# Random-feature attention and a normalised two-layer MLP on one core: tokens centred in place of weights, fp32 weight loads, shared PSUM banks, half-array products and a backward-pass order

## The chip, the cores and the metric

The kernel runs on one core of one Trainium2 chip. The metric is device microseconds (us) from launch to end. Five engines work from lists in fixed order: TensorE (PE; its weight loads are shown as PEld), VectorE (DVE), ScalarE (ACT), GpSimd (POOL) and SyncE (SP, which here only issues DMAs). The lists are made when the program is built. Nothing is reordered at run time: an instruction that waits holds up all that stands behind it on its engine.

## The reference, cut to what matters

```python
def phi(x):                                            # x: (8, 8, 576, 64)
    proj = np.einsum('bhsd,df->bhsf', x, w_phi)        # w_phi: (64, 128)
    proj = proj - np.max(np.abs(proj), axis=-1, keepdims=True)
    return np.concatenate([np.exp(proj), np.exp(-proj)], axis=-1)
q_p, k_p = (phi(q), phi(k))
kv = np.einsum('bhsf,bhsd->bhfd', k_p, v); z = np.sum(k_p, axis=2)
num = np.einsum('bhsf,bhfd->bhsd', q_p, kv)
den = np.einsum('bhsf,bhf->bhs', q_p, z)[..., None] + 1e-06
x = num / den                                          # heads side by side: (8, 576, 512)
xn = (x - mean(x)) / np.sqrt(var(x) + 1e-06) * g_ln
out = x + np.maximum(xn @ w_ch1, 0.0) @ w_ch2          # 512 -> 2048 -> 512
```

## The kernel before, in words

**Attention** goes in 32 units; a unit is two (batch, head) slices. Its 1152 rows are eight tiles of 128 plus a ninth, "mixed", tile that holds the two 64-row tails. For one unit PE transposes k and q into `qkT_ps` (L397, and the mixed tile in L405), multiplies by w_phi into `pm` (L476: four products of 256 columns for k, four for q; the weight is block-diagonal, so that one product serves two slices) and into `px` for the mixed tile (L433, L434). It multiplies q once more with the features on the partitions into `pt` (L543). DVE takes the largest absolute value over the features (L483, L437), ACT the exponentials (L492 for k, L549 for q, L447 and L451 for the mixed tile). POOL scales v by the maxima's exponentials into `vv` (L504 to L513). PE sums `kv` (L571, L576) and `num` (L605, L611). DVE combines the two halves of `num` and inverts the denominator (L618, L624, L628), and POOL writes the quotient into `x` (L634).

**MLP.** Eight units make a pair: two batches with all heads, so 1152 rows of x. A pair goes through the MLP in three blocks of 384 rows: PE transposes x (`xT_ps`, L705), multiplies by `w1` (`hT_ps`, L776, 16 groups of four products per block), ACT or DVE apply the relu (L786, L784; every third group is DVE's by a fixed rule), PE multiplies by `w2` (`ch_ps`, L807), DVE scales by 1/std and adds x (L814), SP stores.

**Mean.** The mean of the layer norm is taken out of the weights: for each quarter n of w1, PE makes the mean over the rows (`mean_ps`, L346), ACT copies it (L353), DVE scales by g and subtracts (L356, L363) and POOL subtracts for two of four row blocks (L368). The transposed x can then be used uncentred.

**Loads.** q, k, v come by SP's queue in fp32. The bf16 transposes read the upper halves of the fp32 words. w1 and w2 come in quarters by POOL's queue, which turns fp32 to bf16 on the way (L310, L320). Each quarter's issue stands on POOL behind the `vv` work of one unit (`behind`).

**PSUM** has eight banks: `ps_A` two buffers of two banks (pm and pt; after pair 0 also qkT_ps and px), `ps_N` one bank (kv, num), `ps_B` three banks (hT_ps, ch_ps, xT_ps, mean_ps; in pair 0 also qkT_ps and px).

**Order.** The program first lists all operations with an engine, an estimated duration, a hand-made rank (a planned start time `V`) and what they read and write. `Order.run` then plays the list through: each engine takes the ready operation of lowest rank. What comes out is the order in which instructions are emitted.

Of the kernel before, what the change touches and what calls it, by code (L numbers as in the profile page):

```python
# [22 lines left out]

class Op:
    __slots__ = (
        "engine", "us", "emit", "rank", "lag", "deps", "users", "acquire", "release",
        "ready", "left", "number",
# [3 lines left out]
class Order:  # L31

# [9 lines left out]
    def add(self, engine, us, rank, emit, r=(), w=(), acquire=None, release=None, lag=0.12):  # L42
        op = Op()
        op.engine, op.us, op.emit, op.rank, op.lag = engine, us, emit, rank, lag
        op.acquire, op.release = acquire, release
        op.number, op.users, op.ready = len(self.ops), [], 0.0
# [11 lines left out]
        return op  # L58

    def run(self):  # L60
        waiting, free, room, events, done = {}, {}, self.room, [], []

        def offer(op):
            heapq.heappush(events, (op.ready, 1, op.number, op))

        for op in self.ops:
            waiting.setdefault(op.engine, [])
            free.setdefault(op.engine, 0.0)
            if not op.left:
                offer(op)  # L70
        now = 0.0
        while events:
            now = events[0][0]
            while events and events[0][0] <= now + 1e-9:
                _, kind, _, op = heapq.heappop(events)
                if kind == 1:
                    heapq.heappush(waiting[op.engine], (op.rank, op.number, op))
                elif kind == 0:
                    if op.release:
                        room[op.release[0]] += op.release[1]  # L80
            for engine, queue in waiting.items():
                if free[engine] > now + 1e-9 or not queue:
                    continue
                passed = []
                while queue:
                    item = heapq.heappop(queue)
                    op = item[2]
                    if op.acquire is None or room[op.acquire[0]] >= op.acquire[1]:
                        break
                    passed.append(item)  # L90
# [3 lines left out]
                if op is None:  # L94
                    continue
                if op.acquire:
                    room[op.acquire[0]] -= op.acquire[1]
                end = now + op.us
                free[engine] = end
                done.append(op)  # L100
                heapq.heappush(events, (end, 2, op.number, op))
                heapq.heappush(events, (end + op.lag, 0, op.number, op))
                for o in op.users:
                    o.ready = max(o.ready, end + (0.03 if o.engine == engine else op.lag))
# [4 lines left out]
        for op in done:  # L109
            if op.emit:  # L110
                op.emit()
# [4 lines left out]
def kernel(  # L116
# [11 lines left out]

# [21 lines left out]
    ST = NT * P  # L150
# [7 lines left out]
    NR = ST // RN  # L158
    NM = RN // P
    NW = 4  # L160
    WC = DH // NW

# [3 lines left out]
    xpool = ctx.enter_context(tc.tile_pool(name="xpool", bufs=NPAIR))  # L166
    moe_sb = ctx.enter_context(tc.tile_pool(name="moe_sb", bufs=2))
    out_pool = ctx.enter_context(tc.tile_pool(name="out_sb", bufs=4))

    ps_A = ctx.enter_context(tc.tile_pool(name="ps_A", bufs=2, space=bass.MemoryType.PSUM))  # L170
    ps_N = ctx.enter_context(tc.tile_pool(name="ps_N", bufs=1, space=bass.MemoryType.PSUM))
    ps_B = ctx.enter_context(tc.tile_pool(name="ps_B", bufs=3, space=bass.MemoryType.PSUM))


    wphi_f = consts.tile([P, F], FP32, name="wphi_f")
    nc.sync.dma_start(out=wphi_f[0:D, :], in_=w_phi)
    nc.sync.dma_start(out=wphi_f[D : 2 * D, :], in_=w_phi)
    gln_sb = consts.tile([P, KC], FP32, name="gln")

    ident = consts.tile([P, P], BF16, name="ident")  # L180
    make_identity(nc, ident)
    nc.scalar.preload_act_table_set("natural_log_exp_and_others")

    wb = {}
    for nm, s0, s1 in (("wbk", 1.0, 1.0), ("wbx", 2.0, 1.0), ("wbq", 2.0, 2.0)):
        wb[nm] = t_ = consts.tile([P, 2, F], BF16, name=nm)
        nc.vector.memset(t_, 0.0)  # L190
        nc.vector.tensor_scalar_mul(out=t_[0:D, 0, :], in0=wphi_f[0:D, :], scalar1=s0)
        nc.vector.tensor_scalar_mul(
            out=t_[D : 2 * D, 1, :], in0=wphi_f[D : 2 * D, :], scalar1=s1
        )
    wbq, wbk, wbx = wb["wbq"], wb["wbk"], wb["wbx"]

    eps_sb = consts.tile([P, 1], FP32, name="eps")
    nc.vector.memset(eps_sb, 1e-6)
    ones = consts.tile([P, P], BF16, name="ones")
    nc.vector.memset(ones, 1.0)  # L200

    qk_bufs, v_bufs = [], []
    for i in range(NBUF):
        qk_bufs.append((
            consts.tile([P, 2, HG, MX * D], FP32, name=f"qk{i}"),
            consts.tile([P, HG, 2, D], FP32, name=f"qx{i}"),
        ))

        vx = consts.tile([P, HG, 2, D1], FP32, name=f"vx{i}")
        nc.gpsimd.memset(vx, 0.0)  # L210
        nc.gpsimd.memset(vx[0:64, :, 0, D:D1], 1.0)
        nc.gpsimd.memset(vx[64:128, :, 1, D:D1], 1.0)
        v_bufs.append((consts.tile([P, HG, MX * D], FP32, name=f"v{i}"), vx))
# [3 lines left out]
    ea_bufs = []  # L217
    for i in range(2):
        eb = consts.tile([P, 2, (MX + 2) * P], BF16, name=f"ea{i}")
        nc.gpsimd.memset(eb[:, :, MX * P :], 0.0)  # L220
        ea_bufs.append(eb)

    w1_sb = consts.tile([P, KC, DH], BF16, name="w1")
    w2_sb = consts.tile([P, JC, DM], BF16, name="w2")

    g_mean = consts.tile([P, KC, P], BF16, name="g_mean")

    sched = Order({"A": 2, "N": 1, "B": 3})
    add = sched.add

    def mm(n, cols):
        return n * (cols / 2.4 + 4.0) / 1000.0


    GBPS = 215.0

    behind = []

    def dma(queue, rank, nbytes, emit, r=(), w=(), us=0.6, lag=2.2):
        r = (*r, *behind)  # L240
        key = ("dma", len(sched.ops))
        add(queue, us, rank, emit, r=r, w=(key, *w))
        add("DMA", nbytes / GBPS / 1000.0, rank, None, r=(key, *r), w=w, lag=lag)

    def load_group(g, rank, units, queues):

        (qk, qx), (vb, vx) = qk_bufs[g % NBUF], v_bufs[g % NBUF]
        pair, hg = divmod(g, NGRP)
        u0, nu = units[0], len(units)
        us = slice(u0, u0 + nu)  # L250

        def rows(t, half, tail):
            if pair == 0:
                b, h0, step = hg // 2, 4 * (hg % 2) + 2 * u0 + half, 2
            else:
                b, h0, step = 2 * pair + half, hg * HG + u0, 1
            run, np_, s0 = (D, 64, 4 * P) if tail else (4 * D, P, 0)
            return bass.AP(
                tensor=t.tensor, offset=t.offset + ((b * H + h0) * S + s0) * D,
                ap=[[run, np_], [step * S * D, nu], [1, run]],  # L260
            )

        def rows_of_pair(t):
            b, h0 = hg // 2, 4 * (hg % 2) + 2 * u0
            return bass.AP(
# [693 lines left out]
```

## Time and profile before

| | |
|---|---|
| median of 2 runs (433.11 and 434.84) | 433.98 us |
| span of the profiled execution, first to last instruction | 431.2 us |
| busy PE, DVE, ACT, POOL in it | 385.5, 302.7, 234.1, 170.8 us |
| mean granted TensorE clock | 0.956 |
| last `ch_ps` product ends | 426.7 us |

The profile has no time of its own for the profiled execution outside its span; the median stands 2.8 us above it, which is taken as what lies around the span. Products of PE overlap in the pipeline: the duration of one runs from its entry to its last result, so what a row of products costs in a full stream is read from the distance between the starts of neighbouring rows.

### The profile page before, as it was taken

To read this page: it belongs to the slowest core of one execution; us is meant where nothing else is said; L and a number is where in the kernel's file an instruction comes from. 1 tells how busy PE (TensorE), PEld (TensorE's weight loads), DVE (VectorE), ACT (ScalarE), POOL (GpSimd) and SP (SyncE) were. 2 spreads that over 40 slices of the span, in tenths; PEclk is the share of its full clock that TensorE was granted. 3 is DMA by queue.
4 is the path that set the end of the run, shared out by engine and by line. 5 is a ranking of instruction groups with operands and counts; after the bars stand their busy time and mean duration, and the time that the engine had idled before them with its cause. 6 is when DMAs were issued, how large, how long until landed. Compare 5 with 4: busy or idle time off the path is not lost.

```text
span 431.2 us, 9039 instructions
## 1 busy us (share of the span) xinstructions
PE 385.5 (89%) x3340; PEld 242.6 (56%) x3392; DVE 302.7 (70%) x727; ACT 234.1 (54%) x513; POOL 170.8 (40%) x345
## 2 busy tenths in 40 slices
PE   3755657899999999799999999999999999999995
PEld 2532533565666666566666666666666655555542
DVE  4787788678878787797687887888778869322222
ACT  1863452777576664666566665577567741522210
POOL 2758674577044354640344444434444520000000
PEclk9985677999999999699999999999999999999999
DMA  5999493375332424511244243510100011101012
GB/s 143 220 271 244 134 228 114 49 120 149 128 110 81 136 87 154 142 53 52 85 123 143 81 135 106 160 55 2 42 34 2 26 49 51 27 24 49 26 49 73
DMA packets 50732, 42.67 MB, mean 99 GB/s; under 512 B 17280, under 2 KB 46080, under 8 KB 50688
## 3 DMA queue, kind: packets, MB, share of 16 engines
q1 hardware_dynamic: 45072, 37.30, 28.2%
q0 software_dynamic: 4224, 4.19, 6.1%
q10 hardware_dynamic: 1392, 0.59, 0.6%
q8 instruction: 26, 0.43, 0.4%
q14 instruction: 18, 0.15, 0.1%
HBM read 36.77 MB, written 9.44 MB: 107 GB/s over the span
## 4 chain that ended last, share of the span: by engine, by line
PE 81%; DVE 6%; ACT 6%; issue 2%; DMA 2%; POOL 2%; SPq 1%; ACTq 0%; DVEq 0%; POOLq 0%
PE hT_ps L776 29%; PE ch_ps L807 27%; PE pm L476 6%; PE kv L576 4%; PE num L605 3%; PE qkT_ps L397 3%; ACT ea_129 L549 3%; PE pt L543 2%; PE xT_ps L705 2%; DVE w_133 L356 2%; PE mean_ps L346 1%; PE kv L571 1%; DVE m L483 1%; ACT EB L492 1%; PE num L611 1%
## 5 line engine op out<-in xcount | busy, mean ns | idle before, releaser
L776 PE MATMUL hT_ps<-xT,w_133 128*128 128x384 bf16 x768 | 148.9, 328 | 4.6 <-DVE hT L784 1.9
L807 PE MATMUL ch_ps<-w_134,hT 128*128 128x512 bf16 x539 | 142.7, 379 | 1.8
L786 ACT ACTIVATE hT<-hT_ps 128x384 bf16<-128x384 f32 x132 | 65.1, 493 | 85.4 <-PE hT_ps L776 85.0
L634 POOL TENSOR_TENSOR x<-numc,rden 128x192 bf16<-128x192 f32 (+3 forms) x112 | 51.3, 461 | 135.6 <-DVE rden L628 125.3
L776 PEld LDWEIGHTS <-w_133 128*128 128x128 bf16 x768 | 73.0, 98 | 55.2 <-issue 6.5
L483 DVE TENSOR_REDUCE m<-pm 128x8 f32<-128x1024 f32 x64 | 77.9, 1218 | 15.3 <-PE pm L476 14.6
L807 PEld LDWEIGHTS <-hT 128*128 128x128 bf16 x576 | 51.9, 98 | 41.7
L784 DVE TENSOR_SCALAR hT<-hT_ps 128x384 bf16<-128x384 f32 x60 | 33.3, 555 | 41.3 <-PE hT_ps L776 41.0
L492 ACT ACTIVATE EB<-pm 128x1024 bf16<-128x1024 f32 x64 | 62.2, 1025 | 0.0
L618 DVE TENSOR_TENSOR numc<-num,em 128x195 f32<-128x195 f32 x96 | 33.9, 353 | 18.9 <-PE num L605 10.3
L814 DVE SCALAR_TENSOR_TENSOR o<-ch_ps,rstd,x 128x512 f32<-128x512 f32 x36 | 26.8, 746 | 19.2 <-PE ch_ps L807 19.2
L549 ACT ACTIVATE ea_129<-pt 128x1024 bf16<-128x1024 f32 x32 | 32.0, 1022 | 11.4 <-PE pt L543 6.0
L549 ACT ACTIVATE ea_131<-pt 128x1024 bf16<-128x1024 f32 x32 | 32.2, 1033 | 7.4 <-PE pt L543 4.9
L624 DVE TENSOR_TENSOR numc<-numc,num 128x195 f32<-128x195 f32 x96 | 33.9, 353 | 1.9
L476 PEld LDWEIGHTS <-qkT 128*128 128x128 bf16 x256 | 24.4, 103 | 14.1 <-issue 5.9
L447 ACT ACTIVATE EB<-px 128x128 bf16<-128x128 f32 x64 | 17.8, 278 | 24.1 <-DVE m L437 22.0
L415 DVE COPY qkT<-qkT_ps 128x1024 bf16<-128x1024 bf16 x32 | 21.8, 681 | 9.6 <-PE qkT_ps L397 9.3
L576 PE MATMUL kv<-vv,EB 128*128 128x65 bf16 x512 | 28.3, 201 | 0.0
L576 PEld LDWEIGHTS <-EB 128*128 128x128 bf16 x512 | 24.1, 103 | 3.7 <-issue 0.5
L728 DVE BATCH_NORM_STATS2 st<-x 128x6 f32<-128x512 bf16 x36 | 24.4, 678 | 0.0
L476 PE MATMUL pm<-wbk,qkT 128*128 128x256 bf16 x128 | 21.3, 294 | 2.8 <-DVE qkT L415 1.1
L476 PE MATMUL pm<-wbq,qkT 128*128 128x256 bf16 x128 | 20.6, 286 | 2.9 <-ACT ea_129 L549 2.2
(95 smaller groups left out, 509.1 us busy)
## 6 DMA issues: line engine op xcount, KB each, us to landing
out_dram<-o SPq DMA_DIRECT2D x32, 256.0 KB, 2.3
qk_108<-in_k_dram SPq DMA_DIRECT2D x10, 256.0 KB, 3.2
v_114<-in_v_dram SPq DMA_DIRECT2D x10, 256.0 KB, 3.3
w_133<-in_moe_w_ch_dram POOLq DMA_DIRECT2D x4, 512.0 KB, 8.0
qk_115<-in_k_dram SPq DMA_DIRECT2D x8, 256.0 KB, 3.4
qk_115<-in_q_dram SPq DMA_DIRECT2D x8, 256.0 KB, 3.2
qk_122<-in_k_dram SPq DMA_DIRECT2D x8, 256.0 KB, 2.9
v_121<-in_v_dram SPq DMA_DIRECT2D x8, 256.0 KB, 2.9
```

Of the source, the lines that this page charges most:

```text
L476: nc.tensor.matmul(ps[:, 2 * c : 2 * c + 2, :], u["qkT"][:, (i * 4 + c) * P : (i * 4 + c + 1) * P], wbk if i else wbq, start=True, stop=True,)
L483: nc.vector.reduce_max(out=u["m"][:, i, 0:MX], in_=u["pm", i], axis=AX.X, apply_absolute_value=True)
L492: nc.scalar.activation(u["EB"][:, t, 0:MX, :], u["pm", 1], AF.Exp, scale=(1.0, -1.0)[t])
L549: nc.scalar.activation(u["EA"][:, t, 0:1024], u["pt"], AF.Exp, scale=(1.0, -1.0)[t])
L576: nc.tensor.matmul(ps[:, t, c // 4, :], EB[:, t, c, :], vv[:, t, c, :], start=False, stop=(t == 0 and c == MX - 1), skip_group_check=True,)
L618: nc.vector.tensor_tensor(out=st["numc"], in0=st["ps"][:, 1], in1=bcast(u["em", 0][:, c0 : c0 + 3], 2, D1), op=ALU.mult,)
L624: nc.vector.tensor_add(out=st["numc"], in0=st["numc"], in1=st["ps"][:, 0])
L634: nc.gpsimd.tensor_tensor(out=dst, in0=st["numc"][ps_, i : i + n, 0:D], in1=bcast(st["rden"][ps_, i : i + n], 2, D), op=ALU.mult,)
L776: nc.tensor.matmul(st["ps"], w1_sb[:, kc, jj * P : (jj + 1) * P], pr["xT"][r][:, kc, :], start=(kc == 0), stop=(kc == KC - 1),)
L784: nc.vector.tensor_relu(h_sb, st["ps"])
L786: nc.scalar.activation(h_sb, st["ps"], AF.Relu)
L807: nc.tensor.matmul(ch[t], hT[r, jj][:, rt * P : (rt + 1) * P], w2_sb[:, jj, :], start=(jj == 0), stop=(jj == JC - 1),)
```

## The change

**Tokens centred.** `mean_ps`, its copy and the centring of w1 go. DVE instead subtracts the mean from each 128-row tile of x (`xc`, L841; 36 of them) once `bn_stats` has given it, and PE transposes xc. The transposes now stand behind the statistics.

**Weights.** The eight quarters come as fp32 by SP's queue into the buffers of x that pairs 2 and 3 use later (`stage`, two of them), and ACT or POOL cast 32 pieces of 128x512 to bf16; those of w1 are multiplied by g on the way. A quarter's load waits for the casts of the quarter two before it.

**Loads of tails.** The 64-row tails of q, k, v come for four or eight units at once, before for one or two. The first DMA is k's main rows, before it was w_phi and tails.

**Mixed tiles** are done once for two units of k, and for two units of q, with products of their own (L400 to L459). In pair 0, where a unit is two heads of one batch, the tails of both batches are joined in one mixed tile in the second half of the pair. The small copies `x<-xs` by DMA go.

**Half-array products.** `pm` is now made by products with 64 rows: each tile of 128 rows is multiplied by the 64x128 w_phi once on the upper and once on the lower half of the array (L543), into different banks. A unit has 16 products of 128 columns, before 8 of 256.

**PSUM.** `ps_A` stays with two buffers of two banks for pm and pt. The other four are one pool of single banks, for all else. `pm` for k and q are one operation after pair 0.

**Engines by choice.** The copies of qkT_ps and xT_ps and all relus may go to ACT or DVE, whichever the planner has free first.

**Ranks.** `Order.due` plays the list backward from the end, by due times; the rank of an operation is its due time less an allowance (8 us for attention, 4 us for transposes and statistics, 0 for the MLP). Durations and delays between engines in the planner are new.

```diff
+        for op in self.ops:
+            op.rank = rank[op.number] - op.early
...
+            nc.vector.tensor_scalar(
+                out=pr["xc", r][:, t % NM, :], in0=x[:, t, :],
+                scalar1=pr["mv"][:, t, 0:1], scalar2=None, op0=ALU.subtract,
+            )
...
+            for i in sides:
+                u["pm", i] = ps = ps_A.tile([P, 2, MX // 2, F], FP32, tag="A", name="pm")
+                for c in range(4):
+                    for e in range(2):
+                        rows = slice(e * D, (e + 1) * D)
+                        nc.tensor.matmul(
+                            ps[:, e, c, :],
+                            u["qkT"][rows, (i * 4 + c) * P : (i * 4 + c + 1) * P],
+                            (wbk if i else wbq)[rows, e, :], start=True, stop=True,
+                        )
...
+                if e == "ACT":
+                    nc.scalar.activation(dst, src, AF.Copy, scale=g)
+                else:
+                    ENG[e].tensor_scalar_mul(out=dst, in0=src, scalar1=g)
...
+    ps_B = ctx.enter_context(tc.tile_pool(name="ps_B", bufs=4, space=bass.MemoryType.PSUM))
...
+    load_w1(0, "SP", 1.6)
+    load_w1(1, "SP", 2.6)
```

Three places in the lists, before and now. On PE, before, between the two halves of the `kv` of unit 2, counted from 0 (x is the attention's result, w_133 is w1, qk_122 the third group of q and k loads, that of units 4 and 5):

```order
L705 MATMUL xT_ps<-ident,x 128x128
L346 LDWEIGHTS g_mean
L346 MATMUL mean_ps<-w_133,g_mean 128x512 [waits DMASW0_49]
...
L571 LDWEIGHTS EB
L571 MATMUL kv<-vv,EB 128x130 [waits Pool_49]
...
L405 LDWEIGHTS qx_123 [waits DMAHW3_49,DMAHW7_49,DMAHW2_49,DMAHW0_49]
L405 MATMUL qxT_ps<-ident,qx_123 128x128
L397 LDWEIGHTS qk_122 [waits DMAHW1_49]
```

and now, where the third group is called qk_84:

```order
L694 MATMUL num<-KV,ea_95 128x65
L513 LDWEIGHTS qk_84 [waits DVE_49,DMAHW5_49]
L513 MATMUL qkT_ps<-ident,qk_84 128x128 [waits PE_49]
...
L658 LDWEIGHTS EBx
L658 MATMUL kv<-vv,EBx 128x130 [waits Pool_49]
...
L513 LDWEIGHTS qk_84 [waits DMAHW6_49]
```

The transposes of unit 4 stood behind two groups of mean products, the `num` of unit 2 and the first half of the `kv` of unit 3; now they stand behind the `num` of unit 1, around the second half of the `kv` of unit 2, and no product waits for w1 there. The first `hT_ps` product stood at row 686 of 6786, when the `pm` of six units were issued; it now stands at row 1054 of 7266, when those of eight units are issued and unit 8 is transposed.

The loads. Before on POOL, a quarter of w1 behind each unit's `vv`:

```order
L513 TENSOR_TENSOR vv<-vx_110,en 128x130
L310 DMA w_133<-in_moe_w_ch_dram 128x4x512
L504 TENSOR_TENSOR vv<-v_114,em 128x8x64
L509 CAST vv<-em 128x8
L513 TENSOR_TENSOR vv<-vx_110,em 128x130
```

and now on SP (x_102 and x_103 are the two staging buffers, qk_83 and v_86 the loads of group 1, those numbered 84 and 87 of group 2, qk_82 of group 3):

```order
L275 DMA qk_83<-in_q_dram 128x2x256
L275 DMA x_102<-in_moe_w_ch_dram 128x4x512
L275 DMA v_86<-in_v_dram 128x2x256
L275 DMA x_103<-in_moe_w_ch_dram 128x4x512
L275 DMA qk_84<-in_k_dram 128x4x256
L275 DMA qk_84<-in_q_dram 128x4x256
L275 DMA kx_90<-in_k_dram 64x4x64 x2
L275 DMA v_87<-in_v_dram 128x4x256
L275 DMA vx_92<-in_v_dram 64x4x64 x2
L275 DMA qx_88<-in_q_dram 64x8x64 x2
L275 DMA qk_82<-in_k_dram 128x4x256
```

The weights are in one queue with q, k and v, and the first half of w1 stands ahead of the loads of units 4 to 7. The casts stand on POOL and ACT between the work of the units:

```order
L614 TENSOR_TENSOR vv<-vx_92,en 128x130
L359 TENSOR_SCALAR w_98<-x_102,gln 128x512 x2
L605 TENSOR_TENSOR vv<-v_86,emk 128x8x64
L610 CAST vv<-emk 128x8
L614 TENSOR_TENSOR vv<-vx_92,emk 128x130
```

A cast that waits for its load holds up the `vv` behind it.

More of the change, by code (lines that the diff above doesn't have):

```diff
@@ L198 @@
[L198 to L213, printed above, removed]
@@ L228 @@
-    sched = Order({"A": 2, "N": 1, "B": 3})
-    add = sched.add
-    def mm(n, cols):
[L232 to L240, printed above, removed]
-        key = ("dma", len(sched.ops))
[L242 to L248, printed above, removed]
+    x_bufs = [consts.tile([P, NT, DM], BF16, name=f"x{i}") for i in range(NPAIR)]
@@ new lines, in tails @@
+        data = []
+        for what in parts:
+            for s in range(n0, n0 + 2) if what == "k" else qheads:
+                data += tail_keys(pair, s, what)
+        key = (g, slot)
+        pool, tag, res = bank(g)
+        wide = ns * 2 * F + (2 * P if qheads else 0)
+        add("PE", mm(ns, 128), V, transposes, r=data, w=[("xT2_ps", key), ("xT2", slot % 2)],
+            acquire=("B", 1))
+        add_any(
+            {"DVE": 0.13 + ns * 0.07, "ACT": 0.1 + ns * 0.11}, V, copy,
+            r=[("xT2_ps", key)], w=[("xT2", slot % 2)], release=[("B", 1)],
+        )
@@ L647, in a_num @@
[L647 to L655 removed]
+                out=dst, in0=st["numc"][:, i : i + cnt, 0:D],
+                in1=bcast(st["rden"][:, i : i + cnt], 2, D), op=ALU.mult,
+            )
+        key, s = ("num", num), num % 3
+        n_mm = sum(2 if c.__defaults__[0] else 1 for c in chunks) * 2
@@ L912 @@
[L912 to L925 removed]
+            w_ = units[n - 1]
```

1093 lines of the change are left out of this document (650 added, 443 removed).

## The prediction

> **What bounds the kernel now.** I read the page's busy times and slices first, then the windows by stage, then the timeline of each stage, and last the chain.
>
> ```profile
> span 431.2 us, 9039 instructions
> PE 385.5 (89%) x3340; PEld 242.6 (56%) x3392; DVE 302.7 (70%) x727; ACT 234.1 (54%) x513; POOL 170.8 (40%) x345
> PE   3755657899999999799999999999999999999995
> PEclk9985677999999999699999999999999999999999
> ```
>
> PE is the busiest engine. The digits show two kernels in one: up to the eighth slice, some 80 us, PE is half idle and for part of it at a reduced clock; from there it is full, except near slice 17. The windows, cut at those stages, say the same (the columns are busy us and count of PE, PEld, DVE, ACT, POOL, then clock, DMA share, GB/s):
>
> ```profile
> 0.00:28.80 28.80, 15.29 (x151) 11.10 (x154) 19.91 (x52) 16.16 (x34) 15.78 (x43) 1.00 0.83 207
> 28.80:47.70 18.90, 10.57 (x82) 6.29 (x82) 13.15 (x28) 6.21 (x12) 14.10 (x24) 0.51 0.82 212
> 47.70:80.00 32.30, 21.54 (x187) 14.31 (x190) 25.70 (x56) 16.79 (x39) 19.73 (x35) 0.81 0.68 160
> 200.00:366.00 166.00, 164.38 (x1527) 104.94 (x1552) 130.98 (x324) 101.08 (x224) 66.61 (x132) 1.00 0.22 71
> ```
>
> From 200 to 366 us PE is busy 99% of the time at full clock. To see whether busy is also full, I read the distance of the starts there:
>
> ```profile
> 324.72 0.61 PE L397 MATMUL qkT_ps<-ident,qk_108 128*128 128x128 bf16 x8
> 325.17 0.81 PE L776 MATMUL hT_ps<-xT,w_133 128*128 128x384 bf16 x4
> 325.82 0.22 PE L571 MATMUL kv<-vv,EB 128*128 128x130 bf16 x1
> 325.88 0.42 PE L576 MATMUL kv<-vv,EB 128*128 128x65 bf16 x8
> 326.13 0.81 PE L807 MATMUL ch_ps<-w_134,hT 128*128 128x512 bf16 x3
> 326.78 0.22 PE L571 MATMUL kv<-vv,EB 128*128 128x130 bf16 x1
> 326.84 0.42 PE L576 MATMUL kv<-vv,EB 128*128 128x65 bf16 x8
> 327.09 0.60 PE L476 MATMUL pm<-wbq,qkT 128*128 128x256 bf16 x4
> 327.53 0.59 PE L543 MATMUL pt<-qkT,wbk 128*128 128x512 bf16 x2
> 327.96 0.33 PE L705 MATMUL xT_ps<-ident,x 128*128 128x128 bf16 x3
> ```
>
> One product follows the next in a distance that goes with its columns: 0.056 us for 128 (325.17 less 324.72, by 8), 0.1625 for 384, 0.217 for 512, 0.11 for 256, 0.031 for 65, 0.06 for 130. So from 80 us on only fewer products, or fewer columns, make the kernel shorter. The start is another matter:
>
> ```profile
> 10.00 2.36 DVE L483 TENSOR_REDUCE m<-pm 128x8 f32<-128x1024 f32 x2
> 25.60 1.23 DVE L483 TENSOR_REDUCE m<-pm 128x8 f32<-128x1024 f32 x1
> 33.40 1.39 DVE L363 TENSOR_SCALAR w_133<-w_133,gln 128x512 bf16<-128x512 bf16 x2
> 41.37 3.14 DVE L356 SCALAR_TENSOR_TENSOR w_133<-w_133,gln,mean 128x512 bf16<-128x512 bf16 x2
> 48.95 1.23 DVE L483 TENSOR_REDUCE m<-pm 128x8 f32<-128x1024 f32 x1 [0.67 <-PE pm L476]
> 65.35 1.44 PE L776 MATMUL hT_ps<-xT,w_133 128*128 128x384 bf16 x4 [1.25 <-DVE xT L711]
> 79.51 1.46 PE L776 MATMUL hT_ps<-xT,w_133 128*128 128x384 bf16 x8 [0.48 <-DVE hT L784]
> ```
>
> The first maxima of units 0 and 3 start at 10.0 and 25.6 us: 5.2 us a unit, with DVE as the pace. The next unit's come at 48.95, after a hole of 23 us in which DVE centres w1 and PE's list is at the mean products, with unit 4's transposes behind them. MLP products start at 65.35 and run without holes from 79.5.
>
> **The change part by part.** I sum the new span in four pieces: up to the first hT product, the products after it, the idle time among these, the end.
>
> *The start.* The mean products, their copies and the centring go, and with them the hole. What remains is the attention's pace. The first load is now k's, so I let the first maximum come 2.5 us earlier, at 7.5. Eight units have their pm before the first hT: 8 x 5.2 = 41.6. Added to DVE in this stretch are three tiles' statistics and centrings and three copies of xT_ps. Their rows, and those that I need below:
>
> ```profile
> L728 DVE BATCH_NORM_STATS2 st<-x 128x6 f32<-128x512 bf16 x36 | 24.4, 678 | 0.0
> L729 DVE BATCH_NORM_AGGREGATE mv<-st 128x2 f32<-128x6 f32 x36 | 6.5, 182 | 1.2
> L363 DVE TENSOR_SCALAR w_133<-w_133,gln x8: 341/447/1252, 33.4 to 71.6; 128x512 bf16<-128x512 bf16 x8
> L786 ACT ACTIVATE hT<-hT_ps 128x384 bf16<-128x384 f32 x132 | 65.1, 493 | 85.4 <-PE hT_ps L776 85.0
> L711 DVE COPY xT<-xT_ps 128x384 bf16<-128x384 bf16 x48 | 16.5, 347 | 6.3 <-PE xT_ps L705 6.2
> L434 PE MATMUL px<-qkT,wbk 128*128 128x128 bf16 x32 | 7.5, 233 | 0.0
> DMA packets 20847, 15.14 MB, mean 189 GB/s; under 512 B 7402, under 2 KB 20840, under 8 KB 20840
> 426.68 0.75 DVE L814 SCALAR_TENSOR_TENSOR o<-ch_ps,rstd,x 128x512 f32<-128x512 f32 x1 [2.48 <-PE ch_ps L807]
> ```
>
> That is 3 x (0.678 + 0.182 + 0.447) + 3 x 0.347 = 5.0 (a centring is the form of L363, whose median I take; its bounds are 0.34 and 1.25, or 1 us less and 2.4 more). By the engines the first hT comes at 7.5 + 41.6 + 5.0 = 54 us. Half of the qkT copies may go to ACT; the casts (six on ACT, ten on POOL in this stretch, no row shows them in this form) fall on engines that were busy 16 of the first 29 us, so I let them cost nothing here; without this cover, six on ACT would be 3 us at the 0.493 of L786, which is the nearest in size.
>
> But the loads now share one queue, in a fixed order: up to the last quarter of w1, whose cast stands on ACT and POOL inside unit 7, SP and ACT issue 14.0 MB (7.1 of q, k and v of pair 0, 4.2 of w1, the rest for units 8 to 11). At the 189 GB/s of the first 80 us (row above) that lands at 74 us, at the 290 of the best ten us before (row under rival b) at 48; behind the cast stand some 6 us of ACT's work before the first hT. So the loads say 54 to 80, the engines 54. I take **62**: nearer the engines, because the rate before included stretches in which the queue waited.
>
> *The products after it.* Behind the first hT the list holds 768 hT (124.8 us at 0.1625), 576 ch (125.0 at 0.217), 896 of 65 columns (27.8), 48 of 130 (2.9), 48 pt (10.4 at 0.217), 363 transposes and px of 128 (20.3), 23 px of 256 (2.5) and 384 pm of 128 (21.5). Sum 335. Only the last group is of a new kind. Before, these 24 units had 192 products of 256 (21.1 us): if the halves ran one after another, nothing would be gained. If two run side by side, a pair costs at least one 0.056, and at most two weight loads with their products as they pass at 65 columns, 2 x 0.031 = 0.062. I take 0.062: 192 x 0.062 = 11.9, or **9.6 less** (bounds 10.8 less and none). The change from whole to half array and back, twice for each of 24 blocks, may cost nothing, or as much as a product stays in the array beyond its distance: 0.233 (L434) less 0.056 = 0.177. I take the middle, 0.1: **4.8** (0 to 8.5).
>
> The Trainium skill (TensorE: Matmul & The Clock Gate, Part 3 on packing small matmuls) has products on different row groups run together, 4 ns apart; its page TensorEngine Tiling (Key Properties) has every change of tiling mode drain the array. No run so far shows either. By both together the two terms would be 10.8 less and 8.5 more, which makes 412 instead of the sum below.
>
> *Idle among them.* Before, from the 25th hT product at 79.51 to the end of the last ch at 426.7 is 347.2 us, for products that add up to 335.0 by the same distances: 12 us idle. Most of it lay between pairs 1 and 2, where x is not yet complete:
>
> ```profile
> 160.00:200.00 40.00, 35.96 (x337) 23.99 (x341) 33.91 (x85) 25.31 (x56) 17.15 (x34) 0.91 0.37 109
> ```
>
> The change puts statistics and centring into that chain, and against it spreads the MLP products by due times: by the distances above, the lists now hold 10 us of MLP products between the first pm of units 15 and 16 and 11 between those of 16 and 17; before they held 2 and none. I take **10** (4 to 18). PE stays the bound there: DVE was busy 131 of 166 us from 200 on (fourth row of the windows); 36 centrings at 0.447 add 16 us to its whole list, and about half of the qkT copies leave it.
>
> *The end* is unchanged: from the last ch to the last instruction 431.2 - 426.7 = **4.5**.
>
> Sum: 62 + 335 - 9.6 + 4.8 + 10 + 4.5 = 406.7 us of span. The profiled execution's span stands 2.8 under the median of the runs shown, so the forecast is **410 us**, 24 less than 434. Where the 24 come from: before, the first hT came at 65.35, the products behind it add up to 342, and 431.2 - 4.5 - 65.35 - 342 = 19 were idle. So the start gives 3, the products that are now ahead of the first hT give 7, the halves 10 less 5, and less idle time 9. The hole of 23 us shows in the second and the last: eight units are through at 62 where six were at 65, and MLP products then find attention work beside them.
>
> **The rivals.**
>
> (a) *The half products don't overlap* and the array drains at each change, so that this part doesn't do what it says: 9.6 + 3.7 more, 423. For it: no row shows two products side by side. Against it: their results go to different banks and their rows to different halves.
>
> (b) *The loads pace the start.* At 189 GB/s the last quarter of w1 lands at 74 and the first hT comes at 80, 18 later: 428. For it: the lists are fixed, a cast that waits on ACT holds up the exponentials behind it, and w2 (17.7 MB up to its first quarter) stands behind as well. Against it: fewer and larger tail loads, and up to 290 GB/s in some stretches of 10 us before:
>
> ```profile
> 20.00:30.00 10.00, 6.07 (x75) 4.38 (x77) 9.45 (x25) 5.79 (x15) 5.69 (x15) 0.96 1.15 290
> ```
>
> (c) *Slower: each half product waits until the one on the other half has left the array.* Its price is the 0.233 us of L434 instead of 0.031 for each of the 384 after the first hT: 77.6 more, less the 4.8 for block changes: 483. It decides from 24/384 = 0.062 us more per product on. For it: 16 changes of half per unit. Against it: before, weight loads already overlap products on the whole array.
>
> (d) *Better:* the loads keep up, the start is 56 and the idle time 4: 398.
>
> **How the numbers follow.** Chances: forecast 0.60, (a) 0.12, (b) 0.15, (c) 0.06, (d) 0.07. A measurement of this kernel tells about 2% from no change, so the borders are 425.3 and 442.7. The forecast with its own bounds, (d) and two thirds of (a) are faster; most of (b) and the rest of (a) are the same; (c), and a tail of (b) with more stalls, slower: 0.80, 0.13, 0.07. The range goes from the sum with its good bounds (54 + 335 - 10.8 + 0 + 4 + 4.5 + 2.8 = 390) to (b) with a little more, 431.
>
> **What would show it.** Right: no hole in the maxima between units 3 and 4; the first hT near 62 us; two pm of 128 columns starting within some 10 ns of each other and eight of them in about 0.25 us; hT and ch at their old distances; PE over 95% busy from 80 us on. Wrong at the start: ACT or POOL waiting for a DMA of x_102 or x_103, or a first hT after 70. Wrong at the halves: eight pm in 0.45 us or more. The forecast as a whole would be wrong if PE had holes of several us between pairs, or if a clock below 1 were granted after 80 us.

## The result and the profile after

The changed kernel took 419.36 us (median of two runs, 419.08 to 419.64) against 433.98 before; the ratio is 0.968, 95% interval 0.960 to 0.977. It is faster, inside the range, and 9.4 us above the 410 that were forecast. The profiled execution took 419.64 us with a span of 417.9, so that 1.7 us lie around the span, where the forecast added 2.8.

The page of the changed kernel, in the rows that were shown of before (PE by slices, then the granted clock):

```profile
span 417.9 us, 9371 instructions
PE 371.7 (89%) x3575; PEld 229.1 (55%) x3632; DVE 274.7 (66%) x705; ACT 268.1 (64%) x569; POOL 171.7 (41%) x336
PE   3657756888999899989999999889999999999995
PEclk9986797999999999999999999999999999999999
```

PE is busy 14 us less in all, and at 89% as before. The first eight slices are no better filled than they were. The windows, at the cuts of before and with the two stretches in which PE still waits, show who is busy instead (busy us of PE, PEld, DVE, ACT, POOL, then clock, DMA share, GB/s):

```profile
0.00:28.80 28.80, 15.63 (x199) 11.04 (x202) 16.85 (x44) 20.11 (x38) 20.83 (x41) 0.94 0.93 266
28.80:47.70 18.90, 13.25 (x166) 9.79 (x167) 16.30 (x46) 16.28 (x36) 16.24 (x32) 0.73 1.09 251
47.70:80.00 32.30, 21.92 (x251) 15.30 (x254) 23.98 (x73) 24.82 (x57) 26.07 (x47) 0.84 0.99 265
140.00:180.00 40.00, 37.21 (x381) 23.28 (x388) 34.51 (x87) 28.71 (x62) 17.52 (x35) 1.00 0.37 113
260.00:280.00 20.00, 16.90 (x174) 10.91 (x175) 18.45 (x50) 16.42 (x38) 8.16 (x16) 1.00 0.21 70
```

The loads now move 251 to 266 GB/s up to 80 us, where they moved 160 to 212. In the third row POOL is the busiest engine, 26 of 32 us; before it was 20 there and DVE 26. The groups of POOL's work up to 67 us say what with (busy us in all, mean ns of one):

```profile
L359 POOL TENSOR_SCALAR w<-x,gln 128x512 bf16<-128x512 f32 x10 | 15.5, 1563 | 1.3 <-DMA x<-in_moe_w_ch_dram 1.3
L718 POOL TENSOR_TENSOR x<-numc,rden 128x64 bf16<-128x64 f32 (+1 forms) x32 | 11.7, 389 | 2.9 <-DVE rden L712 2.9
L605 POOL TENSOR_TENSOR vv<-v,emk 128x512 bf16<-128x512 f32 x8 | 8.4, 1047 | 5.7 <-DMA qk<-in_k_dram 5.6 <-ACT emk L578 0.2
```

The largest row is the ten casts of w1 with the gain multiplied in, at 1.56 us each, in which POOL waited only 1.3 us for loads. The planner has them at 0.62. POOL's timeline just ahead of the first hT shows what such a cast does:

```profile
59.61 0.40 POOL L614 TENSOR_TENSOR vv<-vx,emk 128x130 bf16<-128x130 f32 x1
59.99 3.10 POOL L359 TENSOR_SCALAR w<-x,gln 128x512 bf16<-128x512 f32 x2
63.06 0.54 POOL L718 TENSOR_TENSOR x<-numc,rden 128x64 bf16<-128x64 f32 x2
63.56 1.04 POOL L605 TENSOR_TENSOR vv<-v,en 128x512 bf16<-128x512 f32 x1
```

Two casts stand between the two halves of `vv`. PE's timeline in the same microseconds waits for exactly these halves:

```profile
65.15 0.27 PE L658 MATMUL kv<-vv,EBx 128*128 128x130 bf16 x1 [3.10 <-POOL vv L614]
65.21 0.65 PE L663 MATMUL kv<-vv,EB 128*128 128x65 bf16 x8
65.67 0.40 PE L410 MATMUL px<-wbk,xT 128*128 128x256 bf16 x1
65.86 1.06 PE L513 MATMUL qkT_ps<-ident,qk 128*128 128x128 bf16 x8
66.71 1.49 PE L915 MATMUL hT_ps<-xT,w 128*128 128x384 bf16 x4
```

The wait is 3.10 us, as long as the two casts, and the first hT, forecast for 62, starts at 66.71. The half products, in PE's timeline of the full stretch, are as forecast:

```profile
308.57 0.40 PE L543 MATMUL pm<-wbk,qkT 64*128 64x128 bf16 x8
308.81 0.39 PE L543 MATMUL pm<-wbq,qkT 64*128 64x128 bf16 x8
309.12 0.82 PE L915 MATMUL hT_ps<-xT,w 128*128 128x384 bf16 x4
```

Eight take 0.24 us, 0.060 a pair (0.062 forecast). The single starts in the trace stand 3 to 4 ns apart within a pair and 52 to 53 between pairs.

hT and ch still stand 0.1625 and 0.217 us apart. Set against the terms of the sum (the products counted in the list at the distances of the prediction, pm at 0.030; the end is measured from the last ch):

| | forecast | measured |
|---|---|---|
| start: the first hT | 62 | 66.7 |
| products behind it, halves side by side | 335 - 9.6 = 325.4 | 325.2 |
| block changes | 4.8 | 24 x 0.16 = 3.8 |
| idle among them | 10 | 17.6 (the rest) |
| end | 4.5 | 4.6 |
| span | 406.7 | 417.9 |

0.16 is the two gaps around a block (0.09 and 0.07 at 308.5 and 309.1). What the forecast lacks is in the first and the fourth row, 4.7 and 7.6 us. The fourth is a remainder: besides waits it holds whatever makes PE slower than its distances, such as a lower granted clock.

### The profile page after: what moved, and what is told of

The parts are those of the page before. It is cut to its first block, busy times and chain, and to the rows that moved or that the text cites. A ratio compares the mean times of both kernels' runs of the same rounds, so it can differ in the third digit from the quotient of the medians.

```text
span 417.9 us, 9371 instructions
## 1 busy us (share of the span) xinstructions
PE 371.7 (89%) x3575; PEld 229.1 (55%) x3632; DVE 274.7 (66%) x705; ACT 268.1 (64%) x569; POOL 171.7 (41%) x336
## 4 chain that ended last, share of the span: by engine, by line
PE 69%; DVE 14%; POOL 5%; SPq 4%; ACT 3%; DMA 2%; issue 2%; DVEq 0%; ACTq 0%
PE ch_ps L945 27%; PE hT_ps L915 25%; SPq L275 4%; PE num L694 4%; DVE m L562 4%; PE kv L663 3%; DVE st L834 3%; PE pm L543 3%; PE qkT_ps L513 3%; DVE xc L841 2%; POOL vv L605 2%; PE pt L636 2%; POOL x L718 1%; DMA v<-in_v_dram 1%; DVE numc L700 1%
## 5 line engine op out<-in xcount | busy, mean ns | idle before, releaser
L915 PE MATMUL hT_ps<-xT,w 128*128 128x384 bf16 x768 | 151.9, 327 | 3.6 <-ACT hT L925 1.2
L945 PE MATMUL ch_ps<-w,hT 128*128 128x512 bf16 x536 | 143.8, 379 | 4.3 <-DVE qkT L266 1.6
L718 POOL TENSOR_TENSOR x<-numc,rden 128x192 bf16<-128x192 f32 (+1 forms) x112 | 50.7, 462 | 120.4 <-DVE rden L712 107.3
L915 PEld LDWEIGHTS <-w 128*128 128x128 bf16 x768 | 71.0, 98 | 53.3 <-issue 4.5
L642 ACT ACTIVATE ea<-pt 128x1024 bf16<-128x1024 f32 x64 | 63.1, 1032 | 5.2 <-PE num L694 2.7
L605 POOL TENSOR_TENSOR vv<-v,emk 128x512 bf16<-128x512 f32 x32 | 33.6, 1051 | 54.6 <-issue 29.1
L700 DVE TENSOR_TENSOR numc<-num,emq 128x195 f32<-128x195 f32 (+1 forms) x96 | 33.0, 347 | 29.1 <-PE num L694 21.3
L694 PEld LDWEIGHTS <-ea 128*128 128x128 bf16 x512 | 29.3, 102 | 15.3 <-issue 2.4
L694 PE MATMUL num<-KV,ea 128*128 128x65 bf16 x512 | 33.6, 199 | 2.4 <-DVE qkT L266 0.8
L706 DVE TENSOR_TENSOR numc<-numc,num 128x195 f32<-128x195 f32 (+1 forms) x100 | 33.7, 344 | 1.4
L605 POOL TENSOR_TENSOR vv<-v,en 128x512 bf16<-128x512 f32 x32 | 33.4, 1044 | 0.6 <-DVE rden L712 0.3
L663 PEld LDWEIGHTS <-EB 128*128 128x128 bf16 x512 | 23.9, 103 | 11.9 <-issue 9.0
```

The lines of the kernel that those rows point to most:

```text
L605: nc.gpsimd.tensor_tensor(out=u["vv"][:, t, 0:MX, 0:D], in0=vb[:, uu, :].rearrange("p (c d) -> p c d", d=D), in1=bcast(e[:, 0:MX], 2, D), ...
L642: nc.scalar.activation(u["EA"][:, t, :], u["pt"], AF.Exp, scale=(1.0, -1.0)[t])
L663: nc.tensor.matmul(ps[:, t, c // 4, :], EB[:, t, (c % 2) * 4 + c // 2, :], vv[:, t, c, :], start=False, stop=(t == 0 and c == MX - 1), ski ...
L694: nc.tensor.matmul(ps[:, t, i, :], lhsT, rhs, start=(j == 0), stop=(j == len(terms) - 1))
L700: nc.vector.tensor_tensor(out=st["numc"][:, 0:nch], in0=st["ps"][:, 1], in1=bcast(em_of(), 2, D1), op=ALU.mult,)
L718: nc.gpsimd.tensor_tensor(out=dst, in0=st["numc"][:, i : i + cnt, 0:D], in1=bcast(st["rden"][:, i : i + cnt], 2, D), op=ALU.mult,)
```

## The experiments

Twelve kernels ran in three groups of four, each group beside the kernel before on one chip (433.2, 433.3 and 434.1 us there). A time is a median of four runs. For the comparisons every run is cut as in the table above: **start** is the first hT's time, **idle** the span less start, products behind the first hT, 0.16 us for each block (23 to 27; none with full rows) and 4.6 for the end. The lists of a run decide how many products stand behind its first hT; they are counted there at the same prices.

| run | us | ratio to before, interval | span | start | products behind | idle |
|---|---|---|---|---|---|---|
| changed kernel again | 420.32 | 0.9695 (0.9654 to 0.9736) | 416.9 | 65.5 | 325.2 | 17.8 |
| 1 gains in the copies of xT | 413.27 | 0.954 (0.9504 to 0.9577) | 411.6 | 61.3 | 325.2 | 16.7 |
| 2 full rows | 423.43 | 0.9771 (0.9732 to 0.9809) | 420.7 | 66.4 | 335.2 | 14.5 |
| 3 no centring | 414.68 | 0.9572 (0.9526 to 0.9618) | 413.0 | 66.2 | 325.2 | 13.2 |
| 4 true prices of casts | 413.01 | 0.953 (0.9485 to 0.9575) | 409.5 | 56.8 | 326.5 | 17.8 |
| 5 = 1, six loads fewer | 411.91 | 0.9509 (0.9462 to 0.9557) | 410.6 | 60.3 | 325.2 | 16.7 |
| 6 = 1, centring on POOL | 411.77 | 0.9507 (0.9465 to 0.9548) | 409.3 | 62.1 | 325.2 | 13.6 |
| 7 no backward pass | 439.40 | 1.0133 (1.0081 to 1.0186) | 437.6 | 49.8 | 331.5 | 47.4 |
| 8 = 6, planner told | 405.97 | 0.9336 (0.9284 to 0.9389) | 402.6 | 60.8 | 324.4 | 9.1 |
| 9 halves in another order | 420.63 | 0.9679 (0.9628 to 0.973) | 417.7 | 66.2 | 325.2 | 17.9 |
| 10 kv and num in one bank | 424.19 | 0.9761 (0.9711 to 0.9811) | 421.7 | 53.1 | 330.7 | 29.3 |
| 11 no allowances | 408.56 | 0.9399 (0.9356 to 0.9443) | 406.4 | 52.5 | 328.8 | 16.5 |

**The changed kernel again.** 

> The changed kernel again, beside the runs below on the same chip: 418.5 to 420.5 us, span within 1 us of 417.9, first hT product at 66 to 67.5 us.

 The time and the span (416.9) came so; the first hT was 0.5 us earlier than expected.

**1. The gains out of the casts.**

```diff
 # cast_w1: activation(scale=g) or tensor_scalar_mul(scalar1=g)
+                copy_on(e, dst, src)
 # copies of xT
-                copy_on(e, pr["xT", r][:, kc, :], st["ps"])
+                # ACT: activation(Copy, scale=g); DVE: tensor_scalar_mul(scalar1=g)
```

> The gains g are taken out of the w1 casts and put into the copies of xT, so that POOL's ten casts of w1 in the start are plain casts; every engine's list stays as it is. Theory 1 (POOL's w1 casts pace the start, and the gain multiplied in makes them long): each goes from 1.56 to about 0.64 us, 9 us less on POOL up to the first hT; this comes 4 to 7 us earlier, at 60 to 63 us, and the time falls by about as much, to 413 to 416 us. Theory 2 (the chain of the attention units paces the start and the casts lie beside it): the first hT stays at 66 to 67 us and the time within 1.5 us of the changed kernel. If the cast's length is not from the gain, the ten rows stay at 1.4 us or more and nothing moves.

 The casts became 0.63 us and the time fell by 7 us by the medians (5.3 between the profiled spans):

```profile
L266 POOL CAST w<-x 128x512 bf16<-128x512 f32 x18 | 10.8, 626 | 2.7 <-DMA x<-in_moe_w_ch_dram 2.7
L878 DVE TENSOR_SCALAR xT<-xT_ps,gln 128x384 bf16<-128x384 bf16 x29 | 11.1, 410 | 4.8 <-PE xT_ps L866 4.8
```

The first row holds the ten of w1 and eight of w2; the second is what the gain costs in its new place, 0.06 us more than the plain copy's 0.349 (on ACT 0.58 in place of 0.48). The first hT came at 61.3, 4.2 us earlier, with every list the same. PE's waits for `vv` up to 67 us, in the changed kernel (run again) and in this run, show the path:

```profile
PE kv L658 <- POOL vv L614: 7.2, 7, 3.2
PE kv L654 <- POOL vv L610: 1.9, 2, 1.2
```

From 7.2 us in seven waits they fell to 1.9 in two. Theory 1 holds: the long form of the cast made the start longer. The clock also rose, from 0.84 to 0.93 granted between 47.7 and 80 us; how much of the 4.2 us came by way of it isn't taken apart. The start is now near the forecast's 62, for casts of the length that the planner gave them.

**2. Full rows.**

```diff
-                        rows = slice(e * D, (e + 1) * D)
+                        rows = slice(0, P)
```

> The pm products on half the array are undone alone: the same 16 products of 128 columns a unit and side, but each over all 128 rows, with the half of the weights that is zero; the lists stay. Theory 1 (two half products run side by side, and PE is the bound behind the start): eight go from 0.24 to 0.45 us, 384 products cost 9.6 us more, and some 4 us of block changes go: 5 to 7 us slower, 424 to 427 us. Theory 2 (behind the start PE waits as often as it is busy for what comes from DVE, ACT and POOL, so the halves buy nothing): within 1.5 us of the changed kernel.

 In the full stretch of this run a block lasts 0.90 us:

```profile
298.70 0.61 PE L543 MATMUL pm<-wbk,qkT 128*128 128x128 bf16 x8
299.15 0.61 PE L543 MATMUL pm<-wbq,qkT 128*128 128x128 bf16 x8
299.60 0.23 PE L694 MATMUL num<-KV,ea 128*128 128x65 bf16 x2
```

In the changed kernel it is 16 x 0.030 + 0.16 = 0.64. So the halves save 0.26 us for each of 24 blocks, 6.2 us of PE's work, as theory 1 has it; of the time 3.1 us were seen, between the two theories (the four runs lie at 422.5 to 423.9, those of the changed kernel at 418.7 to 420.7). The rest went into idle time, which was 3 us less with full rows; that PE, with shorter blocks, waits longer for the other engines is the likely reading, and isn't shown wait by wait.

**3. No centring.**

```diff
-            if t % NM == 0:
-                pr["xc", r] = moe_sb.tile([P, NM, DM], BF16, tag="xc", name="xc")
-            nc.vector.tensor_scalar(out=pr["xc", r][:, t % NM, :], in0=x[:, t, :], ...)
+            pr["xc", r] = x[:, r * NM : (r + 1) * NM, :]
```

> Leaves out the subtraction of the mean: the transposes read x itself, and DVE has 36 instructions less; the lists stay otherwise. Theory 1 (the centring lies beside PE's products): 0 to 2 us faster, 417.5 to 419.5, of which about 1 from three centrings ahead of the first hT. Theory 2 (statistics and centring are the chain on which PE waits at the ends of the pairs): 4 us or more faster, 415 or less, with less idle time of PE between 140 and 180 and between 260 and 280 us.

 The windows of this run, at the ends of the pairs:

```profile
140.00:180.00 40.00, 39.88 (x411) 24.78 (x409) 32.36 (x81) 29.37 (x66) 16.13 (x33) 1.00 0.37 116
260.00:280.00 20.00, 18.07 (x192) 11.84 (x190) 14.53 (x37) 16.46 (x38) 7.77 (x16) 1.00 0.11 33
```

PE's 37.21 and 16.90 have become 39.88 and 18.07; the idle time is 13.2 in place of 17.8, and 5.6 us of the time went. Theory 2 holds: not the start (66.2, unchanged) but the ends of the pairs pay for the centring. The forecast had counted it on DVE's whole list, where it does fit, and not in the two stretches in which DVE is busy 34.51 of 40 and 18.45 of 20 us.

**4. True prices of the casts.**

```diff
-                {"ACT": 0.68, "POOL": 0.62}, rank, emit,
+                {"ACT": 0.74, "POOL": 1.56}, rank, emit,
```

> The gains stay in the w1 casts, and only the planner's prices of these are set to what the profile of the changed kernel shows (1.56 us on POOL, 0.74 on ACT, in place of 0.62 and 0.68). The planner then puts 11 of the 16 on ACT and 5 on POOL, where it had 6 and 10, and orders the rest around that. Theory 1 (POOL's 15.6 us of gained casts pace the start): POOL has 7.8 us less and ACT 3.7 more; the first hT comes at 61 to 64 us in place of 65.5 and the time is 414 to 418 us. Theory 2 (whoever casts is late, since ACT is as full as POOL there): the first hT at 65 us or later, 419 us or more.

 413.0 us, a little under what theory 1 gave, and the first hT as early as 56.8. The long form is as long as ever (five of 1.56 us on POOL); with fewer of them on POOL the time is that of run 1. That the order also changes elsewhere is part of it, and the two aren't taken apart: the products ahead of the first hT are 1.3 us fewer.

**5. Six loads fewer.**

```diff
 # load_w1: load=n < 2; load_w2: load=False
-        add(queue, 0.6 if queue == "SP" else 0.4, rank, emit, r=r, ...)
+        add(queue, 0.6 if queue == "SP" else 0.4, rank, emit if load else None, r=r, ...)
```

> On top of the run with the gains in the copies of xT: of the eight loads of weights only the two first are made, and all casts read these two (so it leaves out six loads, 6.3 MB, and computes with wrong weights); the lists of PE, DVE, ACT and POOL stay. Theory 1 (with the casts short, the one queue of loads paces the start, whose share is 1.05 to 1.15 from 20 to 80 us): waits for qk and x of about 8 us go, the first hT comes at 52 to 57 us in place of 61.3, and the time is 404 to 409 us. Theory 2 (the units' own chain of DVE, ACT and POOL paces it): the first hT within 2 us of 61.3 and the time 411 us or more.

 Start 60.3 and 411.9 us beside 61.3 and 413.3: theory 2, and the intervals overlap. The six later loads don't pace the start: without them the DMA share between 47.7 and 80 us is 0.55 in place of 1.12, and the first hT comes 1 us earlier. The run says nothing of the two loads of w1 that are kept. They go out at 10.4 and 11.5 us, ahead of those of unit 4, and the first load left out would go out at 38.3. PE's waits for loads of k are 6.9 us in both runs, all of them before 27 us; two waits of 1.2 us each at 25 and 27, for k and q, remain in run 1. What the first two loads cost there no run shows.

**6. The centring on POOL.**

```diff
-            nc.vector.tensor_scalar(out=..., in0=x[:, t, :], scalar1=pr["mv"][:, t, 0:1], ...)
+            nc.gpsimd.tensor_tensor(out=..., in0=x[:, t, :],
+                in1=bcast(pr["mv"][:, t, 0], 1, DM), op=ALU.subtract)
```

> On top of the run with the gains in the copies of xT: the subtraction of the mean is made by POOL in place of DVE, at the same place in the order; I expect about 1.05 us each there, from the 128x512 product of vv, against 0.35 to 0.42 on DVE. Theory 1 (DVE is the bound where PE still waits, and the 36 centrings cost because they are DVE's): DVE gets 13 to 15 us back, and the time falls by 3 us or more, to 410 or less. Theory 2 (it is the length of the chain from the last x to the first transposes that costs): each of its links is longer on POOL, and the time is 413 us or more.

 A centring takes 1.04 us on POOL; 411.8 us is between the theories, 1.5 under run 1 with intervals that overlap. The idle time fell by 3 and the start rose by 0.8. That fits two costs at once, the load on DVE and the length of the chain, but neither is shown by itself; the old order was not made for this chain.

**7. No backward pass.**

```diff
-        sched.due()
```

> The changed kernel without the backward pass: the ranks stay as the code writes them by hand, everything else as in the changed kernel. Theory 1 (the backward pass is what spreads the MLP products over the units and covers the ends of the pairs): PE is idle 5 to 10 us more after the first hT, above all between 140 and 180 and near 260 us; 424 to 432 us. Theory 2 (the shorter attention chains and the casts do it, whatever the ranks): 417 to 422 us.

 1.3% above the kernel before (1.008 to 1.019). The first hT comes 16 us earlier, at 49.8, and 30 us more are lost behind it:

```profile
140.00:180.00 40.00, 30.47 (x346) 18.98 (x344) 33.23 (x90) 28.26 (x62) 18.32 (x37) 0.87 0.36 115
260.00:280.00 20.00, 9.96 (x134) 6.63 (x131) 18.80 (x55) 14.03 (x33) 8.51 (x17) 0.78 0.31 94
```

In 260 to 280 PE works half the time and DVE 18.80 of 20: statistics, centring and copies of a pair with no MLP products left to cover them. The granted clock is lower too, 0.87 and 0.78 where the changed kernel has 1.00 in both stretches: PE's recorded waits behind the first hT are 27.6 of the 47.4 us, and much of the rest goes with the clock, 0.96 over that whole stretch. Theory 1 holds and its size was too small. With the ranks as written by hand the rest of this change would have brought nothing.

**8. The version the runs point to.**

```diff
 # on top of 6
-                {"ACT": 0.68, "POOL": 0.62}, rank, emit,
+                {"ACT": 0.63, "POOL": 0.63}, rank, emit,
-        add("DVE", 0.25, V, center, r=[("mv", pair % 2, t)],
+        add("POOL", 1.06, V, center, r=[("mv", pair % 2, t)],
```

> The version that the runs point to: the gains in the copies of xT, the centring on POOL, and the planner told of both (1.06 us for a centring on POOL, 0.63 for a cast on ACT or POOL), so that the order is made for them. Theory 1 (the order made with true prices covers the longer centring): faster than the run with the centring on POOL in the old order (411.8 us), 406 to 410. Theory 2 (what is left of PE's waiting is not of the planner's making): 411 to 413 us.

 406.0 us, just under theory 1's range, and the lowest median of all (its interval overlaps that of run 11).

```profile
47.70:80.00 32.30, 27.42 (x300) 18.66 (x302) 27.94 (x81) 28.16 (x63) 25.35 (x54) 0.89 1.11 301
140.00:180.00 40.00, 39.30 (x376) 24.26 (x381) 32.72 (x79) 28.60 (x64) 22.21 (x35) 1.00 0.27 83
260.00:280.00 20.00, 19.07 (x185) 12.06 (x190) 12.99 (x36) 13.16 (x26) 8.21 (x18) 1.00 0.04 14
```

PE is busy 27.42 us between 47.7 and 80 in place of 21.92, at 301 GB/s of loads, and 2 us more at each end of a pair. Start 60.8 and idle 9.1 are close to the forecast's 62 and 10, but in another kernel than the one that was forecast.

**9. The halves in another order.**

```diff
-                for c in range(4):
-                    for e in range(2):
+                for e in range(2):
+                    for c in range(4):
```

> The changed kernel with the eight half products of a side in another order: the four on one half of the rows first, then the four on the other, in place of one here and one there; nothing else moves. Theory 1 (only neighbours on different halves run side by side): eight take 0.42 to 0.48 us in place of 0.24 and the block changes stay: the time is that of full rows (423.4 us) and up to 4 us above it, 423 to 428. Theory 2 (a product over half the rows is short by itself, in any order): 0.24 to 0.28 us for eight, 419 to 421 us.

 Theory 1 is wrong:

```profile
308.37 0.41 PE L543 MATMUL pm<-wbk,qkT 64*128 64x128 bf16 x8
308.61 0.40 PE L543 MATMUL pm<-wbq,qkT 64*128 64x128 bf16 x8
308.94 0.82 PE L915 MATMUL hT_ps<-xT,w 128*128 128x384 bf16 x4
```

Eight take 0.24 us in this order too, and the time is the changed kernel's. But the single starts are other ones: 13 to 19 ns and 37 to 43 ns in turn (53 once at a side's start), in place of 3 to 4 and 52 to 53. Two products per 0.056 us either way. The times are theory 2's, but its reason isn't shown, and the uneven starts don't look like products that are merely short each by itself. The records don't tell on which half a start lies, so whether products of the second half are taken ahead (an exception to the fixed order of the lists), or two on the same half can follow more closely, stays open.

The Trainium skill (TensorE: Matmul & The Clock Gate, Part 3, on the mechanism) has products start and end in program order, and loads of weights overlap products only where the row groups differ. By these two rules together this order should have lost the overlap for six of the seven steps among eight products; the measured 0.24 us doesn't agree.

**10. One bank for kv and num.**

```diff
-    ps_B = ... tile_pool(name="ps_B", bufs=4, ...)
+    ps_N = ... tile_pool(name="ps_N", bufs=1, ...)   # kv, num
+    ps_B = ... tile_pool(name="ps_B", bufs=3, ...)   # the rest
```

> One part undone: kv and num get a pool of one bank of their own again, and the other tiles the remaining three; the planner makes its order for that. Theory 1 (the one pool is worth little, since PE is the bound behind the start): within 3 us of the changed kernel, 418 to 423. Theory 2 (with one bank for kv and num their products wait for DVE and ACT to empty it, at the start above all): the first hT 3 us or more later and 424 us or more.

 The time is theory 2's, though its interval overlaps that of the changed kernel; its mechanism is not: the first hT came 12 us earlier, since the planner made another order, and the loss is behind it, 29.3 us of idle time. PE's waits behind 67 us show num and kv waiting for DVE to empty the bank (us in all, times, longest):

```profile
PE num L695 <- DVE numc L707: 1.5, 3, 1.1
PE kv L659 <- DVE numc L707: 1.5, 1, 1.5
```

That is 3 us of the 11.5 by which the idle time grew. All of PE's recorded waits behind the first hT are 15.5 us, where the changed kernel has 11.1, and the clock between 260 and 280 us is 0.91 in place of 1.00. How much of the rest is the other order and how much the bank was not taken apart.

**11. No allowances.**

```diff
-    E_ATT, E_X, E_MOE = 8.0, 4.0, 0.0
+    E_ATT, E_X, E_MOE = 0.0, 0.0, 0.0
```

> The backward pass stays, and its allowances go (8 us ahead of the due time for attention, 4 for statistics, centring and transposes of x): everything stands at the due time that the planner's prices give. Theory 1 (the 20 us of the backward pass come from the order of the MLP products among the units, the allowances add little): within 4 us of the changed kernel, 418 to 424. Theory 2 (the allowances are what covers the planner's errors, such as the casts of 1.56 us and the loads): holes at the ends of the pairs come back, 428 us or more.

 Both theories fall: 408.6 us, 12 us faster than the changed kernel by the medians, 13 by the ratios (0.9399 and 0.9695). The whole gain lies in the start: the first hT comes at 52.5, with the gained casts still 1.56 us long (seven of them before it on POOL), with 3.6 us more of products behind it and the idle time about the same. In PE's timeline of this run the MLP products start between units:

```profile
52.17 0.40 PE L543 MATMUL pm<-wbk,qkT 64*128 64x128 bf16 x8
52.50 1.47 PE L915 MATMUL hT_ps<-xT,w 128*128 128x384 bf16 x8
53.81 0.22 PE L400 MATMUL xT_ps<-ident,qx 128*128 128x128 bf16 x1
55.04 0.28 PE L410 MATMUL px<-wbq,xT 128*128 128x256 bf16 x1 [1.02 <-DVE numc L706]
```

So the allowances did harm in this kernel. By the code they ask for attention 8 us ahead of its due time, for statistics and transposes of x 4 and for MLP products none, so that attention stands ahead of the first hT and of what it needs; that this is the reason is argued from the code, and no run takes the three apart. That the first hT's time was also a matter of rank, beside the casts' length, was in neither of my accounts. Runs 8 and 11 were not joined.

## Why the prediction was right, and where it was not

**The sign and the bound were right.** The products behind the first hT stand at the distances of the forecast, and neither (a) nor (c) came: eight halves take 0.24 us, and a block change costs 0.08 us. From 80 us to the last ch PE is busy 96% at a clock of 1.00.

**The start was too short by 4.7 us.** The step that failed is the sentence that lets the casts cost nothing because their engines were busy 16 of the first 29 us before. Two things were wrong in it. The price: the nearest row taken, ACT's 0.493, stands for a plain pass, and POOL takes 1.56 us for a cast with a gain per partition (0.63 without). And the cover: not POOL's free share counts, but that the two casts of a stretch stand between the halves of `vv`, for which PE waits in order. Run 1 takes away the price alone and the start comes to 61.3.

**That this is so near 62 is partly luck.** By the engines the sum said 54; the other 8 us were put on for loads. The 5.2 us a unit, read off units 0 to 3 before, held for units 0 to 3 alone (4.7 now). From unit 0 to unit 7 the first maxima come at 6.9 us a unit in the changed kernel and still at 6.5 in runs 1 and 5. The hole between units 3 and 4, which was to go, is 11.9 us in the changed kernel (21.3 to 33.2) and 8.6 in run 1, after 23 before. What makes it once the casts are short is shown in part only: 2.3 us of it in run 1 are the waits for k and q told at run 5. Run 11 shows that the first hT need not wait for eight whole units either.

The Trainium skill (TensorE: Matmul & The Clock Gate, Part 3) has packed products start 4 ns apart, and the trace agrees (3 to 4). The Trainium skill (TensorEngine Tiling, Key Properties) has a change of tiling mode drain the array; the gaps here are 0.09 and 0.07 us, well under the 0.177 at which the forecast bounded a whole drain.

**Rival (b) named a start that comes late, for the most part with the wrong cause.** The loads ran at 251 to 266 GB/s, POOL waited 1.3 us for them before its casts, and leaving six away changed 1 us (run 5). The first two quarters of w1, ahead of unit 4's loads, were not tested.

**The idle time was 17.6 in place of 10,** at the upper end of its bounds (4 to 18). The step that failed is the count of MLP products between the units at the ends of the pairs: the lists hold them, but the chain that they cover grew by the centring, in stretches where DVE is nearly full. Without the centring the idle time is 13.2 (run 3), with the order made for true prices 9.1 (run 8). So the 9 us that I expected from less idle time shrank to 2 (19 before), and this is the larger part of the miss. Even these 2 don't come from shorter waits. PE's recorded waits from the first hT to the last ch are 9.9 us before and 12.6 now (11.1 when run again); what went is time at a lower clock, 0.98 in this stretch before (0.91 from 160 to 200) and 1.00 now.

**Where the 13 us of span came from** by the same account: the start gives nothing (65.35 and 66.7), products that are now ahead of the first hT 7, halves 10 less 4, idle 2. The backward pass makes none of these directly, and still carries them: without it the other parts lose (run 7).

## What to carry to other kernels

Price an operation in its exact form before it goes to an engine with spare time, and look at what stands behind it in that engine's list: ten casts at 1.56 us in place of 0.62 cost 7 us of 420 here. A planner is as good as its prices and its margins: with the gain and the centring moved and their prices mended the kernel is 14 us faster than with the change as it was, and margins of 8 and 4 us ahead of the due times cost 12. An added step on a chain is to be weighed where that chain is the only work, not against an engine's whole list.

## What was not expected of the hardware

A cast of 128x512 from fp32 to bf16 takes POOL 0.63 us, and 1.56 with a factor per partition; ACT takes 0.62 and 0.74 for the two. On DVE the same factor costs a copy of 128x384 out of PSUM 0.06 us (0.349 to 0.410). A subtraction of 128x512 bf16 with a broadcast operand takes POOL 1.04 us. Half-row products of 128 columns come at two per 0.056 us whether neighbours in the list lie on different halves or on the same, with different single starts.
